# Tail scores of a sliding-window attention: row halves of the array trade their products, in another order of all engines

## The chip, the cores and the metric

The kernel runs on one core of a Trainium2 chip. The metric is the device time of one execution in microseconds (us). The engines are TensorE (PE; its weight loads are shown apart as PEld), VectorE (DVE), ScalarE (ACT), GpSimd (POOL), and SyncE (SP), which issues nearly all transfers.

## What is computed

An attention with a sliding window of 128 keys and a linear bias by distance, for 8 batches, 8 heads, 576 positions and a head width of 64; its output, 512 wide, goes through a layer of four causal attention experts of width 64, of which each position takes two. Cut to what matters:

```python
B, H, S, D = 8, 8, 576, 64
scores = scale * q @ k.T                       # per batch and head
mask = (rel >= 0) & (rel < 128)                # rel = query position - key position
scores = where(mask, scores + bias, -1e9)
x = softmax(scores) @ v                        # heads side by side: (B, S, 512)
logits = x @ w_gate                            # 4 experts, 2 taken
for e in range(4):                             # causal attention of width 64
    a = softmax(causal(scale * (x @ wq[e]) @ (x @ wk[e]).T))
    out += weight[e] * (a @ (x @ wv[e]) @ wo[e])
```

## The kernel before

**Groups.** Two heads of one batch are a group g, 32 of them (g = 4 x batch + pair). The first four run in another form (`half_s`, `half_tail` and what belongs to them); groups 4 to 31 run through `attn_s` (scores, softmax, scaling), `attn_t` (transposes of the probabilities) and `attn_pv` (attn·V). Out of the x that comes of it the expert layer computes projections (`qkproj`, `vproj`: tiles wx against WH and WL), causal scores (KKm against QHm, QLm, QJm), transposes, attn·V and the output product.

**Scores of a group.** The head width of 64 is the depth of a score product, so one product takes only 64 of the 128 rows of TensorE's array, and with 64 queries only 64 of its columns. Four such products can stand in the array side by side. The tile `w5` of a group (called `e` in `attn_s`) holds queries and keys of its first head on partitions 0 to 63 and those of its second head on partitions 64 to 127. The unit u = 0 makes two score tiles: `ss[0]`, the first head's, from partitions 0 to 63 (the lower row half of the array), and `ss[1]`, the second head's, from partitions 64 to 127 (the upper one). `products` gives each of them, per tile of 128 queries, two products of 64 queries: against 128 keys for the first query tile and against 192 for the others. The unit u = 1 does query tiles 2 and 3 in the same way.

**The tail.** 576 positions are four query tiles of 128 and a tail of 64. The tail's 64 queries of each head are multiplied with the last whole block of 128 keys and with the 64 keys behind it. In the kernel before, the lower half makes the two products of 128 columns (one for each head) into `ss[0]` and the upper half the two of 64 columns into `ss[1]`, recorded behind the other products of u = 0; a predicated copy on DVE lays the latter over a part of the former, and the tail's block of 128 x 128 goes to the softmax with the blocks of `ss[0]` (`part[0]`). So each half needs queries and keys of the head that the other one holds: `load_hi` fetches them by three small transfers of 64 partitions x 2 x 64, 64 x 128 and 64 x 64 values.

**attn·V.** `attn_pv` too goes by row halves: the keys of a block on partitions 0 to 63 are multiplied on the lower half, those on 64 to 127 on the upper one. Per head the lower half has 3 x 192 + 128 + 64 + 64 = 832 columns, the upper one 3 x 192 + 64 + 64 = 704.

**Order.** All of this is first recorded as a list of operations (`_Rec`). `plan` then writes it out in the order that a table, `ORDER`, gives: for each step the number of an operation and, where an operation may run on one of two engines (copies on ACT or DVE, roundings and scalings on POOL or ACT, subtractions on DVE or POOL), which one is taken. Products that share their place in the array by halves are kept together in pairs (`_pairs`). `place` gives the tiles their buffers, first come, first served, and L1189 issues all of it, so that nearly every instruction has that line. The semaphores follow from the buffers. A buffer number in a name (ps_75, w_84) is thus part of the order too: the same tile may have another number in the other kernel.

Of the kernel before, what the change touches and what calls it, by code (L numbers as in the profile page):

```python
# [19 lines left out]
B, H, S, D = 8, 8, 576, 64  # L20
DM = H * D
E = 4
P = 128
NP_ = H // 2
NQ = S // P
TAIL = S - NQ * P
# [3 lines left out]
SCALE = 1.0 / math.sqrt(D)  # L30
# [8 lines left out]
    "c-p;KeOO#sdB69bckVgKy_*?3v(C6PEBMS*Xc<c?bfFFvTIT7{9onHn1q&8jMnfAOVI35@ObZH?C_IHND7cB6)I>p{5*sSG@RU@dpu{B=Y_N$2g{NSHCKf"  # L39
    "6vY18-Id*=f-Yd`+z<zw#Lk8|GhzQ6bP{@x>q!mqqZIPsVeKYrOmGCYuFQ>%z-v8K{;h(b;Yo><!;<0MQmKgl4wblhq4x~Nh`ed(9xr+Q%|MU6nTiZGR#Z"  # L40
    "7iPxD*~#vIGGwEmPQ9aSsJs_AHUGCP}W}wETDQ)B1~=}&#Lq+yHpktsz@cXQCc6ORm?4aWJCUU#^8l_?ziudJWAZ&%sn)ub$`b*yz8`8vE}BG_JdXMusb-"
    "_LvrcPz*^=+Q*-n*tX%E31QzE??nQ6G{A6)p0ono+`TqQ}Ebzd4q>QgW$6oi`u@mcWhYz0rG9~OWcR>__Q?}BcE`VH^%wa7NJGh{}*LNcb#r-hQI1SJXD@"
    "%}@?-z19r}`|)!^OPGw!CwtMR=M;m~9H0ak(c!JI+!UovE;8Qk%nE&~$#}qJ^-D@_XKeIcEO^yc0qmfHeLfEn-&HM;FW!aB&3Y7=Q{z&=o4{^;Sb2^*IYX"
    "h1AJXoq1V#R<OIki7)M@tD(HCAYo>h@M!b3;N$_Afl2<`F?Myi+*PzQVqx=nFdQllK$hRvGwhnZUo(6;pjecd6JL7ZyleHW`qQW_)#vX9#Y0n$KjVM?qvh"
    "=ohWOD1XFBlLQu{|A*l7v*=m;a!#uT;zA%K4MDn7EeR8cbSFAliQ6xvevp%9<|^8I)tIL_YwsSo!3=DR+e>8F+9YSxbzRSI60O6}loQQOS7F0-58e(pX0q"
    "*AJy5g{3`{l<28O?Hbh`?}AcHxM)BBJ6FS>$Y`wo{yw5=LjKor=K=QoB2JGH$DL&5^)6V#ACJCQ=R9QW?a?9S87rr&Ff@smNQOv4P6V0y1r%g%vS(Z!b@)"
    "-4-buoVe-H#{}HQ!X|<%3%#1fwltLK}dZ!itH9@2#2z9mfZh%xL`j{%zqOj`#a{v!J+v*zBsnEHZxkBB@+9t&^WMNijv8p!OpK^Qd!j+jt!ft=(yEo6lbv"
    "TXBECd~maBX(9X>53Gtv*n^1);J~ruKTo^6=96hhYmupyp-|X(MdS`|D4+gBQ*YncL5%V^-RGm^(zRRTSuZ|8Ub6of@Cm+s8Mvl<1eg6meA`Lgq_T0hV9_"
    "Hem~6jW_XxkG`}5=g&-6=fZ{)!Of55ryl$KXIEFVa<lReKxrb)JJ-qT;=<QfM}H64!M@|MFJAe?r!3h4wSc|mgj&j)x`w{$Gj*E5Y&ENdq+1Gsdc4pB{X_"
    "le+$w<4>tW(v7=);+cH_=gv@KXx)!-<8ph3O%EMbhWE||h^v)2p#BtY1`-ZQmM$I5(5_sXW)<fWd`e&%H5iY<D6<oubuP*&7;al2z~f2VE@SS5SYQ`xo;z"  # L50
# [192 lines left out]
def attn_moe_kernel(ctx, tc, hd, rd, vd, wall, wo, mk, tb, tm, mt, ident, out):  # L243
    nc = _Rec()
# [1032 lines left out]
```

## Time and profile before

| what | us |
| --- | --- |
| median of 3 runs (lowest, highest) | 477.76 (477.13, 478.05) |
| the profiled execution's own time | 478.22 |
| its span in the trace | 476.4 |
| its time around the span | 1.8 |

The span runs from the first to the last instruction in the trace; the execution's own time holds some 1.8 us more around it. The mean granted clock of TensorE in it is 0.996 of full speed. All rows below are of this one execution.

### The profile page before, as it was taken

What the parts mean: (1) busy time and instruction counts of PE and PEld (TensorE: products, weight loads), DVE (VectorE), ACT (ScalarE), POOL (GpSimd) and SP (SyncE); (2) the same over time, 40 slices, a digit from 0 to 9 for tenths busy, and PEclk for the clock granted to TensorE, in tenths of its full rate; (3) what the DMA queues carried; (4) which work ended last, traced back from release to release, by engine and by line L of the source; (5) the groups of instructions that cost most, each with busy time, mean ns of one, the idle gap of its engine ahead of it and who ended that gap; (6) DMA issues with size and microseconds to landing.
All of it is one profiled execution on the core that took longest, in us unless ns stands there. A gap on an engine that the chain in (4) does not pass through costs nothing.

```text
span 476.4 us, 17537 instructions
## 1 busy us (share of the span) xinstructions
PE 468.2 (98%) x6380; PEld 409.5 (86%) x6380; DVE 410.3 (86%) x1900; ACT 371.0 (78%) x1416; POOL 218.2 (46%) x451
## 2 busy tenths in 40 slices
PE   7999999999999999999999999999999999999996
PEld 5888889897889788798898988998889897899875
DVE  6899999989998998879979898898998979975840
ACT  5867978978989577797987989498786968934962
POOL 4713779093826227243381626625163613352440
PEclk9899999999999999999999999999999999999999
DMA  8889333009136026160362047411733030300033
GB/s 200 263 206 225 89 110 80 7 2 221 49 104 141 2 68 192 34 161 1 87 174 68 1 116 192 119 27 38 167 94 102 4 85 2 119 1 1 3 111 111
DMA packets 29861, 44.98 MB, mean 94 GB/s; under 512 B 9424, under 2 KB 15824, under 8 KB 29776
## 3 DMA queue, kind: packets, MB, share of 16 engines
q1 hardware_dynamic: 29040, 43.42, 34.3%
q8 instruction: 50, 0.82, 0.7%
q10 hardware_dynamic: 736, 0.46, 0.4%
q14 instruction: 35, 0.29, 0.2%
HBM read 34.42 MB, written 9.44 MB: 92 GB/s over the span
## 4 chain that ended last, share of the span: by engine, by line
PE 80%; DVE 8%; DMA 4%; ACT 3%; SPq 2%; POOL 2%; issue 1%; DVEq 0%
PE ps L1189 80%; DVE w L1189 5%; ACT w L1189 2%; SPq L1189 2%; POOL w L1189 2%; DMA w<-in_hd 2%; DMA w<-in_rd 1%; DVE ps L1189 1%; DMA w<-in_wall 1%; DVE KKm L1189 0%; DVE r L1189 0%; DVE WL L1189 0%; DVE ALm L1189 0%; DVE mr L1189 0%; ACT QJm L1189 0%
## 5 line engine op out<-in xcount | busy, mean ns | idle before, releaser
L1189 ACT COPY w<-ps 128x512 f32<-128x512 f32 (+3 forms) x230 | 92.9, 449 | 31.1 <-PE ps L1189 20.1
L1189 PE MATMUL ps<-wx,WH 128*128 128x288 f32 (+2 forms) x512 | 110.6, 300 | 0.0
L1189 ACT ACTIVATE w<-w,nm 128x128 f32<-128x128 f32 x252 | 98.8, 395 | 7.5 <-DVE nm L1189 7.3
L1189 POOL TENSOR_SCALAR w<-w,r 128x128 f32<-128x128 f32 x165 | 60.6, 380 | 88.5 <-ACT w L1189 30.5
L1189 POOL TENSOR_SCALAR w<-w,mr,w 128x256 f32<-128x256 f32 (+3 forms) x128 | 78.2, 621 | 43.0 <-DVE mr L1189 15.8
L1189 PEld LDWEIGHTS ps<-wx,WH 128*128 128x128 f32 x512 | 83.3, 189 | 1.5 <-DVE mnm L1189 0.2
L1189 ACT ACTIVATE w<-w,mnm 128x256 f32<-128x256 f32 (+3 forms) x128 | 70.9, 557 | 14.4 <-DVE mnm L1189 13.0
L1189 DVE CUSTOM_DVE_ANT_0 w<-ps,tbt 128x128 f32<-128x128 f32 x288 | 72.5, 283 | 2.9 <-PE ps L1189 2.1
L1189 DVE TENSOR_TENSOR w<-ps,tmt 128x768 f32<-128x768 f32 (+3 forms) x96 | 72.4, 771 | 2.0 <-PE ps L1189 0.9
L1189 PE MATMUL ps<-wx,WL 128*128 128x288 f32 (+2 forms) x256 | 72.0, 296 | 0.0
L1189 PE MATMUL ps<-WH,wx 128*128 128x260 f32 x288 | 62.9, 287 | 0.0
L1189 PE MATMUL ps<-idt,w 64*128 64x64 f32 (+1 forms) x1152 | 60.4, 231 | 1.3 <-POOL w L1189 1.0
L1189 PE MATMUL ps<-w 64*64 64x192 f32 (+3 forms) x1256 | 58.9, 306 | 0.5 <-DMA w<-in_hd 0.4
L1189 PEld LDWEIGHTS ps<-idt,w 64*128 64x128 f32 (+1 forms) x1152 | 48.1, 139 | 11.4 <-issue 3.7
L1189 PE MATMUL ps<-w,vt 64*64 64x192 f32 (+4 forms) x1344 | 56.6, 284 | 0.4 <-ACT w L1189 0.4
L1189 PEld LDWEIGHTS ps<-w,vt 64*64 64x64 f32 (+1 forms) x1344 | 49.7, 133 | 6.5 <-ACT w L1189 1.0
L1189 DVE COPY_PREDICATED ps<-mkt,ps 128x128 f32<-128x128 int32 (+2 forms) x160 | 50.0, 329 | 2.4 <-PE ps L1189 2.0
L1189 PEld LDWEIGHTS ps<-w 64*64 64x64 f32 (+1 forms) x1256 | 45.0, 134 | 7.8 <-DMA w<-in_hd 1.6
L1189 DVE CUSTOM_DVE_ANT_0 w<-ps,mtt 128x384 f32<-128x384 f32 (+2 forms) x96 | 49.8, 551 | 1.0 <-PE ps L1189 0.6
L1189 PEld LDWEIGHTS ps<-WH,wx 128*128 128x128 f32 x288 | 48.4, 190 | 0.7 <-DVE nm L1189 0.2
L1189 PE MATMUL ps<-w,w 128*64 128x64 f32 (+4 forms) x576 | 48.2, 319 | 0.0
L1189 ACT ACTIVATION_READ_ACCUMULATOR w<-w,nm 128x1 f32 x252 | 48.2, 191 | 0.0
(110 smaller groups left out, 944.9 us busy)
## 6 DMA issues: line engine op xcount, KB each, us to landing
w<-in_hd SPq DMA_DIRECT2D x56, 288.0 KB, 4.7
vt<-in_vd SPq DMA_DIRECT2D x28, 320.0 KB, 4.3
out<-w SPq DMA_DIRECT2D x31, 256.0 KB, 2.7
w<-in_hd SPq DMA_DIRECT2D x14, 128.0 KB, 3.6
w<-in_hd SPq DMA_DIRECT2D x56, 32.0 KB, 3.9
w<-in_wall SPq DMA_DIRECT2D x4, 386.0 KB, 5.5
out<-w SPq DMA_DIRECT2D x8, 128.0 KB, 2.3
vt<-in_vd SPq DMA_DIRECT2D x4, 192.0 KB, 4.8
```

Source lines behind the costliest of these rows:

```text
L1189: getattr(getattr(tc.nc, e), m)(*a, **k)
```

## The change

In `attn_s` the two halves trade their tail products: the lower one now makes the two of 64 columns, into `ss[0]`, the upper one the two of 128 columns, into `ss[1]`. The predicated copy goes the other way, and the tail's block joins the blocks of `ss[1]`. In `load_hi` the three small transfers keep their sizes: the one of two pieces now goes to partitions 0 to 63, the other two go to 64 to 127. The table ORDER is another one throughout.

```diff
--- before.py
+++ after.py
@@ -36,79 +36,79 @@
 ORDER = (
-    "c-p;KeOO#sdB69bckVgKy_*?3v(C6PEBMS*Xc<c?bfFFvTIT7{9onHn1q&8jMnfAOVI35@ObZH?C_IHND7cB6)I>p{5*sSG@RU@dpu{B=Y_N$2g{NSHCKf"
...
+    "c-pmi4OAT2b!Jz++w~r*8dX`{p6;D)A8^2i7{-v$Ss23%*pPq+){p}Z*f0SHZ192&4rIZB2_%p}299A2UKB$tIZ`ZqL;{W&ix?*0fCDFJ1`@Oj8`u>yQY<"
...
 )
@@ -387,11 +387,12 @@
         r, vt = loaded.pop(g)
         a = hd[b, p]
         row = a.ap[0][0]
-        src = bass.AP(tensor=a.tensor, offset=a.offset + D * row + NQ * P, ap=[[row, D], [QW, 2], [1, TAIL]])
-        nc.sync.dma_start(r[D:, 2 * S : 2 * S + 2 * TAIL].rearrange("p (a n) -> p a n", a=2), src)
-        t = 2 * QW + S + P + (NQ - 1) * P
-        nc.sync.dma_start(r[:D, 2 * S + TAIL :], a[:D, t : t + P])
-        nc.sync.dma_start(r[:D, 2 * S : 2 * S + TAIL], a[:D, QW + S + P + TAIL : QW + S + 2 * P])
+        k1 = 2 * QW + S + P
+        q1 = QW + S + P + TAIL
+        src = bass.AP(tensor=a.tensor, offset=a.offset + q1, ap=[[row, D], [k1 + NQ * P - q1, 2], [1, TAIL]])
+        nc.sync.dma_start(r[:D, 2 * S : 2 * S + 2 * TAIL].rearrange("p (a n) -> p a n", a=2), src)
+        nc.sync.dma_start(r[D:, 2 * S + TAIL :], a[D:, QW + (NQ - 1) * P : QW + NQ * P])
+        nc.sync.dma_start(r[D:, 2 * S : 2 * S + TAIL], a[D:, NQ * P : S])
         prepped[g] = (None, None, None, vt, r)
 
     def warm():
@@ -418,16 +419,15 @@
         ss = [s_tile(g, u), s_tile(g, u + 3)]
         part = products(ss, 2 * u, [e[:, : NQ * P], e[:, TAIL:S]], e[:, S : 2 * S], tbt[:, p], 5)
         if u == 0:
-            c = slice(3 * P, 4 * P)
             lo, up = e[:D], e[D:]
             x, m = 2 * S, S + (NQ - 1) * P
-            nc.tensor.matmul(ss[0][:D, c], lo[:, NQ * P : S], lo[:, m : m + P], start=True, stop=True)
-            nc.tensor.matmul(ss[0][D:, c], lo[:, x : x + TAIL], lo[:, x + TAIL :], start=True, stop=True)
-            c = slice(3 * P, 3 * P + TAIL)
-            nc.tensor.matmul(ss[1][:D, c], up[:, x : x + TAIL], up[:, x + TAIL : x + 2 * TAIL], start=True, stop=True)
-            nc.tensor.matmul(ss[1][D:, c], up[:, :TAIL], up[:, m + P :][:, :TAIL], start=True, stop=True)
-            nc.vector.copy_predicated(ss[0][:, c], mkt[:, P:], ss[1][:, c])
-            part[0].append((3 * P, tbt[:, p, 4], -SCALE, 4))
+            c, w = slice(3 * P, 3 * P + TAIL), slice(3 * P, 4 * P)
+            nc.tensor.matmul(ss[0][:D, c], lo[:, NQ * P : S], lo[:, m + P :][:, :TAIL], start=True, stop=True)
+            nc.tensor.matmul(ss[0][D:, c], lo[:, x : x + TAIL], lo[:, x + TAIL : x + 2 * TAIL], start=True, stop=True)
+            nc.tensor.matmul(ss[1][:D, w], up[:, x : x + TAIL], up[:, x + TAIL :], start=True, stop=True)
+            nc.tensor.matmul(ss[1][D:, w], up[:, :TAIL], up[:, m : m + P], start=True, stop=True)
+            nc.vector.copy_predicated(ss[1][:, c], mkt[:, P:], ss[0][:, c])
+            part[1].append((3 * P, tbt[:, p, 4], -SCALE, 4))
         for h in range(2):
             wrap(ss[h], 2 * u)
             blocks(g, ss[h], part[h])
```

What the new table moves is shown at three places.

On PE, behind the last products of attn·V of group 7 (`w_92,vt_160`), stand the scores of group 8 (tile `w_84` before, `w_83` after). A row with x2 is two products of one half of the array: the two heads' in attn·V and in the tail, the two query halves' in the other scores. Before, ps_76 and ps_71 are tiles of the lower half, ps_73 and ps_75 of the upper one:

```order
L1189 MATMUL ps_72<-w_92,vt_160 64x64 x2
L1189 MATMUL ps_70<-w_92,vt_160 64x64 x2
L1189 MATMUL ps_76<-w_84 64x192 x2
L1189 MATMUL ps_73<-w_84 64x192 x2
L1189 MATMUL ps_76<-w_84 64x192 x2
L1189 MATMUL ps_73<-w_84 64x192 x2
L1189 MATMUL ps_71<-w_84 64x192 x2
L1189 MATMUL ps_75<-w_84 64x192 x2
L1189 MATMUL ps_71<-w_84 64x128 x2
L1189 MATMUL ps_75<-w_84 64x128 x2
L1189 MATMUL ps_71<-w_84 64x128 x2
L1189 MATMUL ps_75<-w_84 64x64 x2
```

After, ps_75 and ps_72 are tiles of the lower half, ps_69 and ps_71 of the upper one:

```order
L1189 MATMUL ps_70<-w_92,vt_160 64x64 x2
L1189 MATMUL ps_76<-w_92,vt_160 64x64 x2
L1189 MATMUL ps_75<-w_83 64x192 x2
L1189 MATMUL ps_69<-w_83 64x192 x2
L1189 MATMUL ps_75<-w_83 64x192 x2
L1189 MATMUL ps_69<-w_83 64x192 x2
L1189 MATMUL ps_72<-w_83 64x64 x2
L1189 MATMUL ps_71<-w_83 64x128 x2
L1189 MATMUL ps_72<-w_83 64x192 x2
L1189 MATMUL ps_71<-w_83 64x192 x2
L1189 MATMUL ps_72<-w_83 64x128 x2
L1189 MATMUL ps_71<-w_83 64x128 x2
```

The tail's pairs have changed sides: 64x128 ended the lower half's list before (`ps_71`) and 64x64 the upper one's, and now the 64x64 stands on the lower half (`ps_72`) and the 64x128 on the upper one (`ps_71`), both ahead of the other products of their tiles.

On PE, behind the expert scores of batch 0 (KKm), stands attn·V of group 6 (`w_90,vt_155`). Before:

```order
L1189 MATMUL ps_74<-KKm,QLm 128x384
L1189 MATMUL ps_72<-KKm,QLm 128x384
L1189 MATMUL ps_74<-KKm,QHm 128x384
L1189 MATMUL ps_72<-KKm,QHm 128x384
L1189 MATMUL ps_76<-w_90,vt_155 64x192 x2
L1189 MATMUL ps_73<-w_90,vt_155 64x192 x2
```

After:

```order
L1189 MATMUL ps_70<-KKm,QHm 128x512
L1189 MATMUL ps_74<-KKm,QHm 128x512
L1189 MATMUL ps_71<-KKm,QHm 128x384
L1189 MATMUL ps_72<-KKm,QHm 128x384
L1189 MATMUL ps_73<-wx_79,WH 128x320 x2
L1189 MATMUL ps_73<-wx_79,WL 128x320
L1189 MATMUL ps_76<-w_90,vt_155 64x192 x2
L1189 MATMUL ps_69<-w_90,vt_155 64x192 x2
```

Three products of the projections (`wx_79`), of 320 columns each, now stand between the two.

On SP, at the start, the second half of the first groups' inputs (`w_91`) and the tail keys of group 4 (`w_82`, `w_83` before, `w_89` after) are fetched. Before:

```order
L1189 DMA w_91<-in_rd 128x2x320
L1189 DMA w_91<-in_hd 128x2x128
L1189 DMA w_91<-in_hd 64x2x256 x2
L1189 DMA vt_129<-in_vd 128x384
L1189 DMA vt_128<-in_vd 128x384
L1189 DMA w_82<-in_hd 64x64
L1189 DMA w_83<-in_hd 64x2x64
```

After:

```order
L1189 DMA w_91<-in_rd 128x2x320
L1189 DMA w_91<-in_hd 128x2x128
L1189 DMA w_89<-in_hd 64x64
L1189 DMA w_91<-in_hd 64x2x256
L1189 DMA w_89<-in_hd 64x128
L1189 DMA w_91<-in_hd 64x2x256
L1189 DMA w_89<-in_hd 64x2x64
L1189 DMA vt_129<-in_vd 128x384
L1189 DMA w_89<-in_hd 64x1152
```

Two of the three small fetches of the tail have moved ahead of the last piece of `w_91`, the third stands right behind it.

## Rows read from the trace of the kernel before

**Rows 1.** Head of the page: the span, and busy time by engine.
```profile
span 476.4 us, 17537 instructions
...
PE 468.2 (98%) x6380; PEld 409.5 (86%) x6380; DVE 410.3 (86%) x1900; ACT 371.0 (78%) x1416; POOL 218.2 (46%) x451
```

**Rows 2.** Waits of PE: who was waited for: us in total, times, longest.
```profile
PE ps L1189 <- DVE ps L1187: 1.3, 1, 1.3
PE ps L1189 <- POOL w L1189: 1.0, 2, 0.7
PE ps L1189 <- ACT w L1189: 0.4, 1, 0.4
```

**Rows 3.** Waits of PEld, the weight loads, in the same columns.
```profile
PEld ps L1189 <- ACT w L1189: 4.3, 15, 0.7
PEld ps L1189 <- POOL w L1189: 3.4, 12, 0.9
```

**Rows 4.** Timeline of PE, four places: start us, busy us, line, operation, shape, count.
```profile
34.64 1.63 PE L1189 MATMUL ps<-w 64*64 64x128 f32 x40
36.20 1.21 PE L1189 MATMUL ps<-w,vt 128*64 128x64 f32 x18
...
185.85 1.64 PE L1189 MATMUL ps<-w,vt 64*64 64x192 f32 x44
187.42 0.33 PE L1189 MATMUL ps<-idt,w 128*128 128x128 f32 x1
...
258.02 2.39 PE L1189 MATMUL ps<-w 64*64 64x128 f32 x64
261.81 0.54 PE L1189 MATMUL ps<-wx,WH 128*128 128x288 f32 x2
...
414.97 3.07 PE L1189 MATMUL ps<-w,vt 64*64 64x192 f32 x88
417.97 0.33 PE L1189 MATMUL ps<-idt,MPL 128*128 128x128 f32 x1
```

**Rows 5.** Timeline of PE, 202.3 to 203.2 us.
```profile
202.78 0.38 PE L1189 MATMUL ps<-w 64*64 64x192 f32 x2
202.83 0.22 PE L1189 MATMUL ps<-w,vt 64*64 64x64 f32 x2
202.89 0.55 PE L1189 MATMUL ps<-w 64*64 64x192 f32 x8
```

**Rows 6.** Timeline of PE, 62.5 to 67.5 us; in brackets idle time ahead and its releaser.
```profile
62.57 0.45 PE L1189 MATMUL ps<-wx,WH 128*128 128x320 f32 x2
62.86 0.31 PE L1189 MATMUL ps<-wx,WL 128*128 128x320 f32 x1
...
64.90 0.35 PE L1189 MATMUL ps<-KKm,QHm 64*128 64x384 f32 x2
65.61 1.99 PE L1189 MATMUL ps<-w,vt 64*64 64x192 f32 x44 [0.36 <-ACT w L1189]
```

**Rows 7.** Lines by form, POOL: count, busy us, mean ns of one, idle time before.
```profile
L1189 POOL TENSOR_SCALAR w<-w,r 128x128 f32<-128x128 f32 x165 | 60.6, 380 | 88.5 <-ACT w L1189 30.5 <-DVE r L1189 27.4 <-PE ps L1189 14.6
```

**Rows 8.** Timeline of SP (issues of transfers), from 13.5 us.
```profile
14.27 1.96 SPq L1189 DMA_DIRECT2D w<-in_hd  x3
```

**Rows 9.** Chain that ended last, its start: start us, us, what.
```profile
13.84 6.93 DMA w<-in_rd
```

**Rows 10.** Timeline of PE, 27 to 29.9 us.
```profile
27.81 1.95 PE L1189 MATMUL ps<-w 128*128 128x192 f32 x34
```

**Rows 11.** Timeline of POOL, 349 to 358 us.
```profile
352.66 4.21 POOL L1189 TENSOR_SCALAR w<-w,mr,w 128x128 f32<-128x128 f32 x6
```

**Rows 12.** Timeline of PE, 353.5 to 358 us.
```profile
356.39 1.21 PE L1189 MATMUL ps<-idt,w 64*128 64x64 f32 x23 [0.26 <-POOL w L1189]
```

**Rows 13.** Timeline of PE, 70.5 to 75 us.
```profile
71.07 1.64 PE L1189 MATMUL ps<-w,vt 64*64 64x192 f32 x44
...
74.35 0.66 PE L1189 MATMUL ps<-KKm,QJm 128*128 128x288 f32 x3
```

More of the change, by code (lines that the diff above doesn't have):

```diff
@@ new lines @@
+    "&h9YiF?Z-EXG|dr*glp9P4|AVh=C@!F~>>Vmo36%k_aEog)GmiCs9!k^ukyiLk*9WQvmyOtHPmSuzVlo-~I`!N#ho9(|1tRBpZk*nNr&Z1IB358`RIAGPC"
+    "kYmu|tQFWmhfq!LjnB+;vdFbmMi^t(#AtRB#YiqmAx3gqL4>E=$D$K9M;L*(cEHC<01h)>{^Rs$hnC2PmuIld0rVR25N&=JAM_3OSt~&tHB^J?s9)MDOxI"
+    "n9Zk4ZmJsY6lUTKdjH{QjVGdxO#I%=T0O|4BDPVR-kmH4&qfANcB;jzi?oMbK5_xMqwhZ?@>zRaXte7ms*cUM0CnYp3{W64bk)4^$IdAV7$ci~&VRa@Q4v"
+    "chT89Y<zl0!=CLCg*vt4VufQ_}7o{0JKCqR(m|KHRS~ws}VJZg2$Pi8b1jdz7)eYI!V`9B26)RBa7KTf6rKTfu>arF0bYuvBTRqAUBK4Q^3b&XFzJ@Fr@z"
@@ new lines @@
+    "9zkKbRMeIsrLK3Ldt?De|zh<?(URPcDy}#bQrp2-`n1#9NIDm#}`g`C0?khM|qi~0!Ux=pX*2d559PU&^u-Wa+h{@?udds0)0H~Y8aYd!~9^A{GhbA=}YK"
+    "of1uMYs(PPvjRWPS2oWsUmD1oXx}@o7dr^Es#?WOp4B<2syu-L!$Zhx!Ta>}ef|_3eR2yGO{Pw*$kx7#uuEoB;c?FasykbGD<|1t7BvuWBEgo~tY?+e|OG"
+    "Ia&iPh0%rDW3chf9^mI__$nMeJ{%rBWJf3IdATevGflg@V>}|nJFa~C{V&)5zMZVDk*O{i0k{TKC0++ius{A}k^RE;!Y*!Pv~&q|6P<zM4lbFMeq*8~$rq"
+    "KE&Z?(Zn<{(mZN7C2++BqA(-?fe*h|Rx1Z`azg`A4gEE>MGLU#v;Mpz5$O%E^2X{>S7(g?LJst|3Gq7^`PzWU;S(;iMF@R-6FgyBa(A3ki(@j&f_&OZG9-"
@@ new lines @@
+    "zL8@KQ|m+&l)f%+i}#-zL0Fih$2^DzUi&fr#w-_Rj+k<8xU2B%$Lvq7{Aa=%0&tl{nm`VeV%_u{vfOE*-VIK<f80$AT&5_;Oj9*Ua<yrBb;<YQ9OQ?Kn~;"
+    ")hM=jncJx!wspc|Na5i*;nrKQi9Sfxt>Lb=LW4rnz4Q{-d<@d{u-UbK6D+yl!S8kqxV3NRb0U#+gt(8QkmQ_}b78IY%h4(^c8sU?c0M_Y!Bbr1l(UpirzV"
+    "=o8cy`?MZbuO~R#{qCXB*h6G7=&@OuLKkW*BJ)*LK_S33IA!ba-KU!{wqhrN!CW<)zh!I3zC-va5FKy>i{_*ypK%H6TaD&@Rk5f!6=^IxR~mss);o&dR9M"
+    "Xq<%IhrqTm@bs0t2AXb%%W;k45E$xcyQ(tP33~anwD<S5_7>`Ue0U-86Hc9y`l9?SNKcOE-a-cfg!7qImj`z5Uwj=_HvUHc9TMee8DtJhyIDm!J9^KXT7v"
@@ new lines @@
+    "17`kL~ue+!gf{oFsoW_nZuoB$ABl-dBn78>i&Y0#x>m81#~TFXiQI@DHy>(LvZ%=pN&b%rB4L3a^q#OSdkGpjK60n9$?$v;S_nsI1Q#<pP}9s^hY=;-*!c"
+    "EmHgja$4Kpoa{yCf!|wFQ;x6)B036g5%i*Rz%2ct^~g#m*&~7_W1C`d=Pnj;Os0dIBLIEeIEhqL2?xuCrUji%+FPeDdhF_0$G@KX8w<tzEb+FhmfhWCqG3"
+    "Uq`pDhxjNI(T;pQLH(|_NdKTazJo=8phBxLs<^0JB?7RhgF7Nl{12p|3e9f!JT`~GwAKyl}hkF3{3*JNRM=~L+>$_Iwn`5`uVFR<|?`Lj~-kcn!hn{t|J+"
+    "sJ8VEe|GKJ@JP_otT}Hz#&B*mJJb#65_VzxN5g7TVjU9_Vfd)f`bj`pFZQ5}3#6?Md&u48;Y;%0T+Ou?4fYmW|bUGD8-zK-JeTc5)+Xd}Ez0mM(7GNZejt"
@@ L112 @@
+    "fqZnDI#XOXytgI6FfuGsm&hTG4$}7iYz4Zf8=bMS0fteQzYr9wn+b<u73sfV!uW"
 )
```

127 lines of the change are left out of this document (55 added, 72 removed).

## The prediction

> **What bounds the kernel now.** I read the head of the page first. In a span of 476.4 us PE is busy for 468.2 us (98%), while POOL is busy for 46% [rows 1]. Then I read who keeps PE waiting: the longest entry of its list, 1.3 us in one wait, lies before the first product; behind it come 1.0 us for POOL and 0.4 us for ACT [rows 2]. The list for the weight loads, which mostly run behind products, adds 4.3 us for copies of ACT and 3.4 us for scalings of POOL, in 27 waits [rows 3]. So the time is that of the work on PE, in the order in which it stands there; another engine counts only where PE catches up with it. A change can pay in two ways: the products themselves take less time on PE, or one of these few waits goes. It can cost by making new ones.
>
> **How long the products of half the array take.** Scores and attn·V of a group use 64 of the 128 rows of the array at a time, and two streams run side by side: the lower half (rows 0 to 63) and the upper half. The next product that takes all rows has to wait for both. I looked up stretches that hold nothing but such products, and took their length from the start of the first to the start of the next full one [rows 4]. By the code, the scores of one group have 128 + 192 + 192 + 192 + 128 = 832 columns on the lower half and 768 on the upper; attn·V of one group has 832 and 704.
> - Scores of one group, 34.64 to 36.20: 1.56 us.
> - attn·V of one group, 185.85 to 187.42: 1.57 us.
> - attn·V of two groups, 414.97 to 417.97: 3.00 us.
> - Scores of one group, the first unit of a second one, and attn·V of one, 258.02 to 261.81: 3.79 us; 832 + 448 + 832 = 2112 columns below, 768 + 384 + 704 = 1856 above.
>
> From the second and third, 832 columns more below cost 1.43 us, which is 1.72 ns per column with 0.14 us to begin and end. The fourth would then be 2112 x 1.72 ns + 0.14 = 3.77 us (measured 3.79), and the first 1.57 (measured 1.56). Had the upper half set the time, 704 columns more would cost 1.43 us, 2.03 ns each, the first would be 1.57 + 64 x 2.03 ns = 1.70 and the fourth 3.91. So the longer half sets the time, and before the change that is always the lower one: attn·V leans on it by 128 columns and the tail of the scores by another 64.
>
> **The change part by part.** *The tail products.* The lower half gives up 64 columns per tail and the upper half takes them. In a stretch without attn·V this only swaps which half is longer. Where attn·V stands in the same stretch, the longer half gets shorter by 64 columns, 64 x 1.72 ns = 0.110 us. I counted both orders on PE: each has 60 stretches of half-row products between full ones. Of the 28 tails, 7 stand in a stretch without attn·V, before as after. Of the other 21, two meet an attn·V whose last products stand in another stretch, so that half of the excess is missing there and the tail only turns it round. 19 tails remain: the longer halves of all stretches sum to 19 x 64 = 1216 columns less. If all of it shows, that is 19 x 0.110 = 2.09 us.
>
> Whether all of it shows depends on how far the halves can run apart. In 12 of the 19 the tail stands ahead of the attn·V that it makes up for: the lower half is simply done earlier and takes the next product, which is next in order anyway. In 7 it stands behind: the upper half must have run ahead of the lower one by the time the tail comes. A row shows that it can: at 202.78 two score products start, the others not before 202.89, while the lower half is still at attn·V (202.83) [rows 5]. The order on PE names the two of the lower half first, so the two early ones are those of the upper half, 0.11 us ahead of their turn. How much of such a lead lasts through a whole group no row shows; between 0 and 0.110 us I take half, 0.055. The sum is 12 x 0.110 + 7 x 0.055 = 1.70 us, with the ends 1.32 (no lead lasts) and 2.09 (all of it).
>
> The Trainium skill has a rule on either side. "TensorE: Matmul & The Clock Gate", The mechanism, says that products start and end strictly in the order of the program, whatever tile they use; by it the 7 give nothing and the sum is 1.32. "TensorEngine Tiling (Array Packing)", Key Properties, says that tiles operate independently; by it the sum is 2.09. The rows at 202.78 speak against the first as a strict rule.
>
> *The wait of attn·V at 65.61.* PE starts the last score product of batch 0 at 64.90 and then sits idle for 0.36 us until the copies of group 6's transposes are there [rows 6]. In the new order three products of 320 columns stand in this place. Two of them took 0.29 us (62.57 to 62.86) [rows 6], so three cover 0.44 us, which is all of the idle time. They are taken from where PE did not wait, so I count 0.36 us of gain; the lower end is 0, should the copies be later by as much.
>
> *The fetches and the rest.* The three tail fetches keep their sizes (16, 32 and 32 KB); only partitions and offsets change. Likewise the predicated copy keeps its 128x64 shape, and the tail's block moves from the first score tile's list to the second's with the same instructions. All of it lies beside PE, and costs nothing so long as PE's rows above stay without a wait on DMA or DVE. *Engines.* POOL gets 13 instructions more, 12 of them scalings that ACT did: 12 x 0.380 = 4.6 us [rows 7] on an engine that idles for 54% of the span. DVE and ACT lose 6 and 7. That, too, costs nothing on average; what it can cost at a place is a rival below.
>
> *The start.* On SP, two small tail fetches of group 4 now stand ahead of the last piece of the first groups' inputs. Three issues took 1.96 us [rows 8], so two are 1.3 us, and the last piece, the third of that row, moves from about 15.6 to 16.9. The slowest transfer there took 6.93 us [rows 9], which puts its landing at 23.8 at the latest. Before, the products on it started inside the row of 27.81 [rows 10]; by the order they now stand some 2 us of PE work earlier, at about 26. The cover is 2 us; without it PE would wait for each us by which the landing is later. I take 0.
>
> Sum: 478.22 (this profiled execution) - 1.70 - 0.36 = 476.16 us. The median of the runs is 0.46 below this execution, so I forecast **475.7 us**.
>
> **The rivals.** *Strict order between the halves.* No lead lasts, and the 7 tails behind give nothing: 477.76 - 1.32 - 0.36 = 476.1. For it: the lead at 202.78 is only 0.11 us, and nothing shows it later. Against it: the same rows. Chance 0.18. By the first rule of the Trainium skill named above this is the case to come.
>
> *New waits take the gain back.* The order of all engines is another one, and PE catches up at other places. Before, ACT and POOL held up products and weight loads for 9.1 us in 30 waits, 0.3 us each [rows 2, 3]. Four to six more of them cost 1.2 to 1.8 us: 476.9 to 477.5, not to be told from before (a difference under 0.2%, 0.96 us, is none that a measurement of this kernel tells). For it: the slack of transposes and attn·V behind their copies is small in both orders. Against it: the sequence of large blocks on PE is nearly the same. Chance 0.20.
>
> *POOL's queue holds up the transposes: slower.* POOL works in order, and a transpose waits for the last scaling of its block. At 352.66 six scalings in a row took 4.21 us [rows 11], and PE came to wait for them at 356.39 [rows 12]. With 12 scalings more in the queue this would have to happen at ten further places of 0.3 us each before 2.06 us of gain turn into a loss of 0.96 us; from 3.0 us of new waits on, the kernel is slower, around 479. For it: POOL is the engine that gets more work. Against it: it idles half the time, and ahead of the same transposes the new order leaves out two of the long roundings. Chance 0.08.
>
> *Waits go elsewhere too.* If one us of the remaining waits goes as well, 474.7. Chance 0.09.
>
> **How the numbers follow.** The forecast has 0.45 and its own range is 475.2 to 476.3, strict order 0.18, waits that eat the gain 0.20, slower 0.08, a larger gain 0.09. Faster by over 0.2% means below 476.8: 0.45 + 0.18 + 0.09 = 0.72. Within 0.2%: 0.20. Slower: 0.08. The range leaves out the slower case and about half of the larger gain, and takes in that of new waits: 474.5 to 477.7.
>
> **What the profile after would show.** The tail: the stretch near 71 to 74 us, attn·V of group 7 and scores of group 8 (3.28 us before [rows 13]), gets shorter by about 0.1 us, and stretches of scores alone keep 1.56 us. The sum over all such stretches falls by 1.3 to 2.1 us at an equal number of products. The wait at 65.61: no idle time of PE ahead of attn·V of group 6. The start: no wait of PE on these fetches between 24 and 30 us. Wrong would be the forecast if the half-row stretches keep their lengths (then the halves are bound to each other), or if PE's list of waits on ACT, POOL or DMA grows by more than 1 us.

## The result and the profile after

| | before | after |
| --- | --- | --- |
| median of 5 runs, us (those of before beside the change) | 477.13 | 472.78 |
| lowest, highest | 476.61, 478.05 | 471.57, 474.09 |
| profiled execution, us (its span) | 478.22 (476.4) | 473.2 (471.4) |

The ratio is 0.9915, with an interval of 0.9896 to 0.9933: the change is faster by 4.35 us. The forecast was 475.7, a gain of 2.06; the result lies below its range. The sign was right; the size that was forecast was half of what came.

First the head of the page of the changed kernel, which answers to [rows 1].

```profile
span 471.4 us, 17542 instructions
...
PE 462.7 (98%) x6380; PEld 403.8 (86%) x6380; DVE 409.3 (87%) x1894; ACT 370.5 (79%) x1409; POOL 222.7 (47%) x464
```

PE is as full as before, with the same 6380 products: its busy time fell by 5.5 us and the span by 5.0. The time was thus not won in idle time of PE that the profile lists as such. Next the waits of PE after the change, in the columns of [rows 2].

```profile
PE ps L1189 <- DMA w<-in_hd: 1.7, 3, 0.7
PE ps L1189 <- DVE ps L1187: 1.3, 1, 1.3
PE ps L1189 <- POOL w L1189: 0.9, 2, 0.5
PE ps L1189 <- DVE w L1189: 0.4, 1, 0.4
```

The wait for ACT is gone. PE's wait for fetched inputs of the scores (DMA) has grown to 1.7 us in three pieces; before it was

```profile
PE ps L1189 <- DMA w<-in_hd: 0.4, 2, 0.2
```

The longest of the three after the change stands ahead of a tail product, in the timeline of PE around 284 us:

```profile
284.45 0.60 PE L1189 MATMUL ps<-w 64*64 64x128 f32 x10 [0.67 <-DMA w<-in_hd]
```

The waits of the weight loads after the change, as in [rows 3]:

```profile
PEld ps L1189 <- POOL w L1189: 3.4, 11, 0.7
...
PEld ps L1189 <- DMA w<-in_hd: 2.7, 6, 0.8
PEld ps L1189 <- ACT w L1189: 2.4, 9, 0.4
```

Those for ACT fell from 4.3 us in 15 to 2.4 us in 9; POOL's stayed, in spite of its 4.5 us more work. The whole list did not fall: leaving out "issue", it sums to 18.5 us before and 20.9 after.

Last the places that the prediction named, in the timeline of PE after the change:

```profile
33.20 1.64 PE L1189 MATMUL ps<-w 64*64 64x192 f32 x40
34.77 0.44 PE L1189 MATMUL ps<-w,vt 128*64 128x128 f32 x4
...
63.03 0.31 PE L1189 MATMUL ps<-wx,WL 128*128 128x320 f32 x1
63.27 1.47 PE L1189 MATMUL ps<-w,vt 64*64 64x192 f32 x28
...
68.96 1.58 PE L1189 MATMUL ps<-w,vt 64*64 64x192 f32 x42
...
71.97 0.40 PE L1189 MATMUL ps<-wx,WH 128*128 128x288 f32 x1
```

Scores alone take 34.77 - 33.20 = 1.57 us, as before [rows 4]. attn·V of group 6 starts at 63.27 with no idle time in brackets ahead of it, where it waited 0.36 us [rows 6]. attn·V of group 7 with the scores of group 8 takes 71.97 - 68.96 = 3.01 us, where it took 74.35 - 71.07 = 3.28 [rows 13]: 0.27 less, not 0.1.

To see where the time went I cut PE's whole course into the 60 stretches of products that use 64 rows at a time (scores, attn·V, and the transposes and causal scores that stand among them; these are the stretches of the prediction) and the rest, each from its first start to the next one's. These sums are made from all starts in the trace, in us. The last four are kernels of the experiments below.

| kernel | stretches of 64 rows | the rest | together |
| --- | --- | --- | --- |
| before | 171.2 | 299.5 | 470.7 |
| after | 167.2 | 298.8 | 466.0 |
| before, with fillers (e4) | 170.8 | 298.5 | 469.3 |
| after, with fillers (e8) | 166.0 | 298.3 | 464.3 |
| e8, tail widened (e12) | 167.5 | 298.7 | 466.2 |
| before, only the tails traded (e1) | 172.8 | 299.8 | 472.6 |

The stretches got 4.0 us shorter; 1.3 to 2.1 was forecast. The profiled execution of before also lost about a microsecond at its start to a halved clock, which is not in that of e4; the two filled kernels are therefore the cleaner pair: 4.8 us out of 5.0 lie in the stretches, and the rest of PE's work takes what it took.

### The profile page after: what moved, and what is told of

The parts are those of the page before. It is cut to its first block, busy times and chain, and to the rows that moved or that the text cites. A ratio compares the mean times of both kernels' runs of the same rounds, so it can differ in the third digit from the quotient of the medians.

```text
span 471.4 us, 17542 instructions
## 1 busy us (share of the span) xinstructions
PE 462.7 (98%) x6380; PEld 403.8 (86%) x6380; DVE 409.3 (87%) x1894; ACT 370.5 (79%) x1409; POOL 222.7 (47%) x464
## 4 chain that ended last, share of the span: by engine, by line
PE 84%; DMA 5%; SPq 3%; DVE 3%; ACT 2%; POOL 1%; issue 1%; DVEq 0%
PE ps L1189 84%; DMA w<-in_hd 4%; SPq L1189 3%; DVE w L1189 2%; ACT w L1189 2%; POOL w L1189 1%; DMA w<-in_wall 1%; DVE ps L1189 1%; DVE WL L1189 0%; DVE ALm L1189 0%; ACT AHm L1189 0%; DVE mr L1189 0%; DVE nm L1189 0%; POOL QJm L1189 0%; DVE ALTm L1189 0%
## 5 line engine op out<-in xcount | busy, mean ns | idle before, releaser
L1189 ACT COPY w<-ps 128x256 f32<-128x256 f32 (+2 forms) x232 | 92.4, 443 | 29.8 <-PE ps L1189 21.3
L1189 POOL TENSOR_SCALAR w<-w,r 128x128 f32<-128x128 f32 x177 | 64.6, 378 | 68.3 <-PE ps L1189 25.4
L1189 ACT ACTIVATE w<-w,mnm 128x512 f32<-128x512 f32 (+3 forms) x128 | 71.2, 558 | 10.0 <-DVE mnm L1189 9.4
L1189 PE MATMUL ps<-WH,wx 128*128 128x260 f32 x288 | 61.5, 285 | 0.0
L1189 PE MATMUL ps<-idt,w 64*128 64x64 f32 (+1 forms) x1152 | 58.6, 230 | 1.0 <-POOL w L1189 0.9
L1189 PE MATMUL ps<-w,vt 64*64 64x192 f32 (+3 forms) x1344 | 56.3, 283 | 0.0
L1189 PEld LDWEIGHTS ps<-w 64*64 64x64 f32 (+1 forms) x1256 | 44.0, 134 | 8.6 <-DMA w<-in_hd 2.7
L1189 DVE CUSTOM_DVE_ANT_0 w<-ps,mtt 128x256 f32<-128x256 f32 (+2 forms) x96 | 49.8, 551 | 0.8 <-PE ps L1189 0.4
```

The lines of the kernel that those rows point to most:

```text
L1189: getattr(getattr(tc.nc, e), m)(*a, **k)
```

## The experiments

My theory after the result: the tail products give what was forecast, and the other half of the gain is time in which PE stands inside its stretches because another engine's data or buffer is late, which the new order takes away. The rivals: the tail is worth twice my price; the gain comes from the start; it comes from the clock.

**e4_fill and e8_after_fill: the clock.** PE had been idle in part between 10 and 12 us. Filler products of 256 columns, whose result nobody reads, are put there, six before and five after. In the table's entries (operation, engine chosen; -2 is a filler), that of before:

```diff
 (79, 0)
+-2
 (78, 0)
+-2, -2, -2, -2
 (82, 0), (110, 0)
+-2
```

> Before, with six more filler products (128x256, results unused) on PE between the first three transposes, 9.5 to 11.3 us, where PE has nothing to do; no other instruction moves. If the idle time ahead of it is why the clock falls: the clock stays at 1.0 from 10 to 16 us and the time is 477.1 - 1.6 = 475.5 us. If the clock falls for another reason, or costs nothing there: 477.1 us, or up to 0.3 us more where the fillers delay the transposes.

> The changed kernel with five more filler products on PE between the first three transposes, as in e4_fill. In 2 of 5 runs of the change the granted clock was 0.996, which in runs of before goes with about 1.1 us more. If that is the same fall of the clock at the start: no run at 0.996, the median at 472.0 to 472.5 us. If it comes from elsewhere: 472.8 us and the same spread.

Measured: e4 476.76 us, ratio 0.9993 (0.9984 to 1.0002); e8 471.57, ratio 0.9882 (0.9869 to 0.9895). The windows of 2 us in the kernel before, with busy time of PE, PEld, DVE, ACT and POOL, the granted clock, the share of the DMA engines and GB/s:

```profile
10.00:12.00 2.00, 1.14 (x5) 0.83 (x5) 1.79 (x16) 1.84 (x10) 1.88 (x6) 0.90 0.80 230
12.00:14.00 2.00, 2.00 (x13) 1.67 (x14) 1.38 (x8) 2.00 (x11) 0.72 (x2) 0.50 1.01 331
```

The same windows of e4:

```profile
10.00:12.00 2.00, 1.73 (x13) 1.52 (x13) 1.93 (x17) 1.88 (x10) 1.99 (x6) 1.00 0.85 255
12.00:14.00 2.00, 2.00 (x39) 1.68 (x37) 1.74 (x14) 2.00 (x11) 0.75 (x3) 1.00 0.90 293
```

With PE busy for 1.14 of the 2 us, the granted clock of the next window was 0.50 (1.2 GHz of 2.4) and PE got through 13 products; with 1.73 busy it stayed at 1.00 and got through 39. But this fall is in some executions only: e4 is no faster than the median of before, since most executions of before lack it (last section). So the clock explains how widely the runs of one kernel lie apart, and not the gain: between kernels without the fall it is 476.76 - 471.57 = 5.2 us. (The two ran beside different runs of before, with medians of 476.89 and 477.07.) e8 is faster than both kernels.

**e12_wide: the price of the tail.** In e8 the two lower tail products get 128 columns again, 64 of which nobody reads; order, engines and fetches stay (the predicated copy reads the 64 that count). The lower half is then as long as before the change.

```diff
-nc.tensor.matmul(ss[0][:D, c], lo[:, NQ * P : S], lo[:, m + P :][:, :TAIL], ...)
-nc.tensor.matmul(ss[0][D:, c], lo[:, x : x + TAIL], lo[:, x + TAIL : x + 2 * TAIL], ...)
+nc.tensor.matmul(ss[0][:D, w], lo[:, NQ * P : S], lo[:, m + TAIL : m + P + TAIL], ...)
+nc.tensor.matmul(ss[0][D:, w], lo[:, x : x + TAIL], lo[:, x : x + 2 * TAIL], ...)
```

> The change with fillers (e8_after_fill, 471.57 us), the same order, buffers and results, but the lower half's tail products have 128 columns again, of which 64 are junk that nobody reads. The longer halves of all stretches grow by 1216 columns, back to before's sum. If the halves run apart freely: 471.6 + 2.1 = 473.7 us. If a tail behind attn·V gives nothing: 472.9 us. If the tail's columns lie beside other work: 471.6 us.

Measured: 473.18 us, ratio 0.9915 (0.9901 to 0.9929), 1.61 more than e8. In the table above the stretches grow by 1.5 us. Two of them in the timeline of PE in e8:

```profile
68.61 1.58 PE L1189 MATMUL ps<-w,vt 64*64 64x192 f32 x42
...
71.61 0.40 PE L1189 MATMUL ps<-wx,WH 128*128 128x288 f32 x1
...
253.67 0.99 PE L1189 MATMUL ps<-w 64*64 64x64 f32 x24
...
257.21 0.40 PE L1189 MATMUL ps<-wx,WH 128*128 128x288 f32 x1
```

and in e12:

```profile
68.82 1.58 PE L1189 MATMUL ps<-w,vt 64*64 64x192 f32 x42
...
71.83 0.40 PE L1189 MATMUL ps<-wx,WH 128*128 128x288 f32 x1
...
254.78 0.99 PE L1189 MATMUL ps<-w 64*64 64x128 f32 x24
...
258.53 0.40 PE L1189 MATMUL ps<-wx,WH 128*128 128x288 f32 x1
```

The second stretch holds two tails and grows from 3.54 to 3.75 us, 0.10 for each. The first holds one, behind all of attn·V, and keeps its 3.00. Over all stretches, start by start: the seven tails without attn·V change nothing (0.00 each). Of the 12 that stand ahead, 11 change their stretch by 0.09 to 0.10. Of the 7 counted as behind, four have the last products of attn·V still to come (per head 128 columns on the lower half and 64 on the upper one) and give 0.10 to 0.11 as well; the one with nothing of attn·V behind it gives 0.00, like the two whose attn·V ends in another stretch. (Three share a stretch with another stall, and can't be read.) So the rival that the tail is worth twice the price falls.

**e1_tail and e2_order: one half of the change each.** e1 keeps the table of before and trades only the tails, with the fetches and the predicated copy; e2 has the table of the change with the tails of before. In each one copy on ACT stands earlier, since a score tile lives longer there.

```diff
+nc.vector.copy_predicated(ss[1][:, c], mkt[:, P:], ss[0][:, c])
...
+            if u == h == 0:
+                blocks(g, ss[1], [(3 * P, tbt[:, p, 4], -SCALE, 4)])
```

(e1; it leaves the tail's softmax steps where they stood, behind the first head's.)

> The order of before, with only the tail products of the two halves traded (the tail's softmax block stays at its place in the order, and one copy on ACT stands earlier, since a score tile now lives longer). The sum of the longer halves falls by the same 1216 columns as in the change. If the halves run apart freely: 477.1 - 2.1 = 475.0 us, and the attn·V and scores stretch near 71 us falls from 3.28 to about 3.05 us. If they start strictly in the order of the program: 475.8 us. If the tail gives nothing by itself and the whole gain of the change is in its order: 477.1 us. The start to 16 us stays as before in each case, with the granted clock at half in 12 to 14 us.

> The changed order with the tail products of before (one copy on ACT stands earlier, since a score tile lives longer). If the tail is worth 2.1 us, the order alone has the other 2.2 us of the 4.35: 474.9 us, with the granted clock at 1.0 through the first 20 us. By the prediction's own steps the order is worth 0.36 us: 476.8 us. If order and tail need each other: above 477.

Measured: e1 479.72 us, ratio 1.0053 (1.0041 to 1.0065); e2 479.00, ratio 1.0044 (1.0029 to 1.0058). Both are slower than before, though together they make 4.35 us of gain. The waits of the weight loads in e1:

```profile
PEld ps L1189 <- ACT w L1189: 5.2, 18, 0.7
PEld ps L1189 <- DVE nm L1189: 3.9, 13, 0.7
```

The entry for `nm`, a small tile that DVE makes out of the scores in a step of the softmax, is new at that size: as I read it, products wait until DVE has read a score tile and its buffer is free. The stretches grew by 1.6 us where the tails alone should have cut 1.6, so some 3.2 us of standing came in (against e4 it is 3.6). The waits of PE in e2:

```profile
PE ps L1189 <- DVE KKm L1189: 1.7, 1, 1.7
...
PE ps L1189 <- DVE nm L1189: 1.3, 5, 0.3
```

Here too DVE is late, but mostly elsewhere: e2's stretches sum to 169.4 us, 1.4 less than e4's, and the rest to 302.1, 3.6 more. So the new order shortens the stretches with the old tails too, and loses more outside them. Neither half of the change gains by itself.

**e3_start: the start.** Before, with its first 141 steps in the order of the change; 111 of them move.

```diff
-(10, 0), (19, 0), (18, 0), (7, 0), (16, 0)
+(4, 0), (9, 0), (7, 0), (12, 0), (10, 0)
```

> Before, with only the operations of its first 141 steps (on PE up to the second half's scores of groups 0 and 1, about 16 us) put in the relative order that they have in the change. Theory of the clock: in the profile of before the granted clock is at half from about 11.6 to 14.9 us, which costs 1.6 us; in the new start it stays at 1.0, so 477.1 - 1.6 = 475.5 us, and the scores at 13.93 take 1.46 us in place of 1.97. Theory of the prediction (the start gives 0): 477.1 us, whatever the clock does, since the start waits for data.

Measured: 476.95 us, ratio 0.9999 (0.999 to 1.0008). The start gives nothing and takes nothing.

**e5_mirror, e6_unmirror and e7_mid: other orders of the softmax steps.** e5 is e1 with the softmax steps of the two heads traded as well, in 283 entries of the table; e6 does the reverse to e2; e7 is before with the 543 entries of the steps from 45 to 81 us in the order of the change.

```diff
-(431, 0), (424, 0), (440, 0), (449, 0)
+(424, 0), (431, 0), (440, 0), (449, 0)
```

(e5 against e1, the first place.)

> The order of before with the tail products traded, as in e1_tail, but the softmax steps of the unit's two score tiles trade places in the order too, so that the tile which holds the tail keeps the place, and so the lifetime of its buffer, that it had in before. Theory of the lifetimes (what e1_tail lost, it lost in waits for score buffers that are read longer, and the shorter half of the array is a gain): 476.9 - 2.1 = 474.8 us if the halves run apart, 475.6 us if they start strictly in the program's order, with waits on DVE as in before. Rival (trading the halves costs by itself in before's order): 479 us or more, as e1_tail.

> The changed order with the tail products of before, as in e2_order, but with the softmax steps of the unit's two score tiles traded in place, so that the lifetimes of the buffers stay those of the change. If the tail is worth 2.1 us in this order too: 472.8 + 2.1 = 474.9 us, so that the order alone keeps 2.0 us of the gain. If the order without the tail is worth nothing, or costs: 477 us or more. If the tail is worth nothing: 472.8 us.

> Before, with only the operations between 45 and 81 us (steps 545 to 1101) put in the relative order that they have in the change; tail products as before. From the two profiles: the time beyond what the products need falls from 3.7 us in that part to 2.4 us, so 476.9 - 1.3 = 475.6 us. By the step of the prediction (only the wait of 0.36 us goes): 476.5 us. If what is saved there comes back later: 476.9 us.

Measured: e5 479.67 us, ratio 1.0057 (1.0044 to 1.0071); e6 475.78, 0.9965 (0.9952 to 0.9979); e7 481.19, 1.0074 (1.0058 to 1.0089). In all three the new places put the step that reads the softmax sums ahead of the exponentials that make them, for 13 blocks in e5, 8 in e6 and 1 in e7, so that these kernels leave out a wait that the others have. Their times therefore decide nothing on the tails, and nothing below rests on them.

**e9_mid, e10_late and e16_last: which part of the program.** Before with fillers, with the change's order, choice of engines and traded tails in one part: e9 from 45 to 81 us (groups 6 to 8), e10 from 81 us to the end (groups 9 to 31), e16 from 216 us (groups 19 to 31).

```diff
+SWAPPED = (9, 10, 11, 12, 13, 14, 15, 16, 17, 18, 19, 20, 21, 22, 23, 24, 25, 26, 27, 28, 29, 30, 31)
...
+        if g in SWAPPED:
```

(e10; the new lines of the tail stand under it, the old ones under `else`.)

> Before with the six fillers of e4_fill (476.76 us), and with the part from 45 to 81 us as the change has it: the operations of steps 545 to 1101 in the change's relative order, and the tail products of groups 6, 7 and 8, which lie wholly inside, traded. The longer halves fall by 2 x 64 columns there, 0.22 us. If the stalls of PE in that part go as the two profiles show it (3.7 us beyond what the products need, 2.4 us after): 476.8 - 0.2 - 1.3 = 475.3 us. By the step of the prediction (only the idle time of 0.36 us goes): 476.2 us. If it comes back later: 476.8 us.

> The complement of e9_mid: before with the fillers, and everything from 81 us on as the change has it, with the tail products of groups 9 to 31 traded. The longer halves fall by 17 x 64 columns, 1.87 us if all of it shows. With the stalls that the profile of the change with fillers lacks from 100 us on (1.6 us): 476.8 - 1.9 - 1.6 = 473.3 us, and e9_mid and e10_late together make the 5.2 us between e4_fill and e8_after_fill. By the prediction (the tails alone, 17 of its 19): 475.2 us.

> e10_late with a later border: before with fillers up to 216 us, from there on the change, with the tails of groups 19 to 31 traded (10 x 64 columns of the longer halves). If the gain is spread evenly over the stretches: tails 10 x 0.085 to 0.110 us, 0.9 to 1.1, and some 1.0 us less of stalls, 474.6 to 474.9 us. If it hangs on one place between 81 and 216 us: 475.8 us or more.

Measured: e9 481.17 us, ratio 1.0085 (1.007 to 1.0101); e10 473.07, 0.9912 (0.9899 to 0.9926); e16 475.40, 0.9966 (0.9954 to 0.9977). e9 misses: it is 4.4 us slower than e4. At its first seam, where one order passes into the other, PE stands for 2.0 us, as its timeline shows; the rest of the loss was not followed:

```profile
47.96 0.33 PE L1189 MATMUL ps<-idt,w 128*128 128x128 f32 x1 [1.43 <-ACT w L1189]
48.82 0.41 PE L1189 MATMUL ps<-wx,WH 128*128 128x320 f32 x1 [0.53 <-ACT w L1189]
```

The other two have one seam each. Against e4 e10 gains 3.7 us and e16 1.4, and e8 gains 1.5 beyond e10. Of the 5.2 us, 1.5 lie before 81 us, 2.3 between 81 and 216, and 1.4 behind. By e12 a tail that counts gives 0.10: 17 such tails stand behind 81 us and 10 behind 216. That leaves about 2.0 us of other gain behind 81 us, 0.4 of it behind 216, and 1.4 before 81, where one such tail stands. It is not at one place. How it divides behind 81 us is rough: what the seams of e10 and e16 cost is not known, e16's runs lie 1.6 us apart, and its median stands between the two cases that were expected.

**e11_three: the gap at attn·V of group 6.** Before with fillers; only the three products of 320 columns (891 to 893) move from ahead of the causal scores to the gap that the prediction wanted them to fill, and the two reads of their result (894, 895) with them.

```diff
 (1028, 0)
-(891, 0), (892, 0), (893, 0)
 (1029, 0)
-(894, 0), (895, 0)
 (685, 0), (686, 0), (684, 0), (681, 0), (679, 0), (683, 0), (680, 0), (682, 0)
...
 (750, 0), (751, 0), (752, 0)
+(891, 0), (892, 0), (893, 0)
```

> Before with the fillers, and with only the three 320-column products moved behind the scores of batch 0, ahead of attn·V of group 6 (the two reads of their result move behind them). By the prediction's step the idle time of 0.36 us goes: 476.4 us. If the new neighbours only move the wait, since the scores ahead of it come earlier by as much: 476.8 us. If the stall is the 0.6 us between the starts beyond a product's own time: 476.2 us.

Measured: 478.51 us, ratio 1.0028 (1.0017 to 1.0039), 1.75 more than e4. The timeline of PE in e11:

```profile
63.92 0.44 PE L1189 MATMUL ps<-KKm,QHm 64*128 64x384 f32 x1 [0.42 <-ACT w L1189]
64.64 0.56 PE L1189 MATMUL ps<-wx,WH 128*128 128x320 f32 x2
65.04 0.31 PE L1189 MATMUL ps<-wx,WL 128*128 128x320 f32 x1
65.28 0.54 PE L1189 MATMUL ps<-w,vt 64*64 64x192 f32 x4
66.39 0.39 PE L1189 MATMUL ps<-w,vt 64*64 64x192 f32 x4 [0.57 <-DVE KKm L1189]
```

The three products came where they should, and attn·V starts behind them without a wait. But 0.42 us of waiting for ACT now stands ahead of the last causal scores, and attn·V waits behind its first products, 0.57 us for DVE's step on KKm. That step is the second of the two moved reads: DVE does it at 65.84 us in e11. So part of the new waiting is made by the edit. The run shows that three products in the gap gain nothing in before's order; it does not show what keeps this place clean in the change.

**e13_eng_after, e14_eng_before and e15_evac_after: the choice of engines.** The two tables differ in the chosen engine of 307 operations: 150 copies out of PSUM (72 from ACT to DVE, 78 the other way), 118 scalings (53 from POOL to ACT, 65 back), 31 roundings and 8 subtractions. e13 is e8 with before's choice in all of them, e15 with before's choice in the 150 copies, e14 is e4 with the change's choice.

```diff
-(82, 1), ... (104, 1), ... (106, 1)
+(82, 0), ... (104, 0), ... (106, 0)
```

(e13, the first three of 307.)

> The change with fillers (471.57 us), every instruction at its place in the order, but each of the 307 copies, roundings, scalings and subtractions for which the change takes another engine than before goes to the engine that it had in before. If the choice of engines is what spares PE its stalls (in the lists of waits the weight loads wait 4.3 us for ACT before and 2.4 us in the change): 471.6 + 1.9 to 3.2 = 473.5 to 474.8 us. If the order alone spares them: 471.6 us. If order and choice fit only together: above 475 us.

> The reverse: before with fillers (476.76 us), the order and the tails as they are, with the change's choice of engine for the same 307 instructions. If the choice by itself spares the stalls: 476.8 - 1.9 = 474.9 us or less. If the order alone does: 476.8 us. If they fit only together: above 477.5 us.

> As e13_eng_after, but only the 150 copies out of PSUM go back to the engine (ACT or DVE) of before; the 118 scalings and 31 roundings stay as in the change. PE waits for these copies, not for the roundings: if the choice counts, this run has most of what e13_eng_after loses. If the scalings count (12 more of them on POOL): 471.6 us.

Measured: e13 532.66 us, ratio 1.1176 (1.1161 to 1.1192); e14 549.49, 1.1523 (1.1507 to 1.1539); e15 504.76, 1.0589 (1.0574 to 1.0603). The waits of PE in e13, and then in e14:

```profile
PE ps L1189 <- POOL w L1189: 13.2, 12, 2.6
PE ps L1189 <- ACT w L1189: 7.2, 5, 2.7
```

```profile
PE ps L1189 <- ACT w L1189: 12.7, 11, 3.4
PE ps L1189 <- POOL w L1189: 12.3, 8, 5.6
```

The same work, in the same order, on engines that are busy for 46 to 87% of the span in e4 and e8, costs 33 to 73 us more when the choice does not belong to the order. Part of this is PE's clock: its mean granted share was 0.98 in the profiled execution of e13, 0.97 in e14 and 0.99 in e15. e13 and e14 come out as order and choice fitting only together, and e15 with about half of e13's loss; none says what share of the change's gain the choice has.

## Why the prediction was right in sign and wrong in size

**The tail products: right in size, one term of it by luck.** The sum was 1.70 us, with 1.32 and 2.09 as its ends; e12 measures 1.6 by the medians and 1.5 by the stretches. The rule behind it (the longer half sets the time) holds stretch by stretch: 0.00 where attn·V is absent, 0.10 for a tail that counts (0.110 forecast). The half price for the 7 tails behind attn·V stood for a lead of the upper half that lasts in part. No run shows such a lead. Of attn·V's 128 columns of excess on the lower half, 64 lie in its last products, and six of the 7 tails have these still to come: they stand ahead of what they make up for, like the 12. The seventh ends the stretch near 71 us, the place that I had named for the reader; it gave nothing, and the 0.27 us there are a stall that went. So the term came right in sum by luck. The Trainium skill's "TensorE: Matmul & The Clock Gate", The mechanism, has products start and end strictly in the order of the program; the tail that ends its stretch agrees with it (3.00 us in e8 and 3.01 in e12), and the four others can't speak against it, since the lower half's excess comes after them. What does speak against it as a rule for single starts is the 0.11 us of [rows 5]. The 1.32 us worked out from it had counted all 7 as giving nothing.

**The waits: the step that failed.** "They are taken from where PE did not wait, so I count 0.36 us of gain" was the only stall in the sum, and of the engines it said "That, too, costs nothing on average". Measured, the gain besides the tail is 5.2 - 1.6 = 3.6 us in the kernels with fillers. The term for stalls was too small by a factor of ten. Two things were wrong in how I came to it.

The first is how I read the profile. I took the waits of the weight loads to run mostly behind products. In stretches of half-row products many of them do not. Here is attn·V of group 6 in e4, first in the timeline of PE, then in that of PEld:

```profile
64.30 1.99 PE L1189 MATMUL ps<-w,vt 64*64 64x192 f32 x44 [0.37 <-ACT w L1189]
66.22 0.79 PE L1189 MATMUL ps<-idt,w 64*128 64x64 f32 x16
```

```profile
64.30 0.19 PEld L1189 LDWEIGHTS ps<-w,vt 64*64 64x64 f32 x4 [0.69 <-ACT w L1189]
64.86 1.28 PEld L1189 LDWEIGHTS ps<-w,vt 64*64 64x64 f32 x40 [0.37 <-DVE w L1189]
```

The 0.37 us ahead of 64.30 are listed for PE. But the group then takes 66.22 - 64.30 = 1.92 us where it needs 1.57: the weights of its fifth product were late by 0.37 us, and PE counts as busy meanwhile. The same 44 products in e8:

```profile
62.95 1.68 PE L1189 MATMUL ps<-w,vt 64*64 64x192 f32 x44
64.56 1.04 PE L1189 MATMUL ps<-idt,w 64*128 64x64 f32 x17
```

They take 1.61 us with no wait ahead: 0.37 + 0.31 = 0.68 us gained where I had counted 0.36. Another such place is attn·V with the transposes behind it, where POOL was late [rows 12]. In e4:

```profile
352.72 1.64 PE L1189 MATMUL ps<-w,vt 64*64 64x192 f32 x44
354.42 0.28 PE L1189 MATMUL ps<-idt,w 64*128 64x64 f32 x2
354.95 1.21 PE L1189 MATMUL ps<-idt,w 64*128 64x64 f32 x23 [0.26 <-POOL w L1189]
355.92 0.51 PE L1189 MATMUL ps<-wx,WH 128*128 128x288 f32 x2
```

and in e8:

```profile
348.29 1.64 PE L1189 MATMUL ps<-w,vt 64*64 64x192 f32 x44
349.86 1.51 PE L1189 MATMUL ps<-idt,w 64*128 64x64 f32 x25
351.12 0.52 PE L1189 MATMUL ps<-wx,WH 128*128 128x288 f32 x2
```

3.20 us became 2.83, again more than the 0.26 in brackets. The better reading was at hand before: set each stretch against the price per column from clean ones, and the difference is the standing time, whoever the list names. The clean stretches give 0.14 us to begin, 1.72 ns per column of the longer half for scores and attn·V, 0.98 ns per column of a half for transposes and 0.47 ns for causal scores. By these prices the stretches behind 20 us stand 6.9 us above their price in e4, 3.7 in e8 and 3.3 in e12. e12 has the columns of e4 in the order of the change and with its choice of engines, so these two together take away 3.6 us of standing time. That is the size of the gain besides the tail.

Three stretches of e4, at 53.17, 61.93 and 352.72 us, hold 2.75 of its 6.9 us, and in them the weight loads waited 2.6 us for ACT, DVE and POOL. There the standing time and the waits for late data are about equal. For the rest the cause is argued from these three: the list of the weight loads as a whole, without "issue", sums to 17.7 us in e4 and 19.2 in e8, so many of its waits must have cost nothing.

The second thing is the engines. I took the net numbers of the order's counts (12 scalings more for POOL), but 307 operations change engine, in both directions. That is no small edit: taken alone it costs 61 to 73 us. What share of the 3.6 us hangs on it no run shows. "*New waits take the gain back*" and "*Waits go elsewhere too*" were priced at a third of a microsecond a wait and one microsecond in all; the second of them was the case that came, with 0.09.

**The mechanism at 65.61: not shown.** The wait is gone in the change, but in e11 the same three products in the gap come with other waits (0.42 and 0.57 us) and a loss of 1.75. So even the 0.36 us rest on a step that no run bears out.

**The fetches and the start: right at the start, incomplete behind.** e3 shows nothing at the start, as counted. Not foreseen were the longer waits for fetches later on (1.7 us in three where before had 0.4, the longest ahead of a tail product). In the profile of e8 they come to 0.7 in two, so they do not belong to every execution. The sign that I had set for a wrong forecast was PE's waits on ACT, POOL or DMA growing by over 1 us: those on DMA did, by 1.3, while the three together grew from 1.8 to 2.6. It was no good sign, for the time fell by more than was forecast. POOL's queue, the slower rival, did not come: PE waits for POOL for 0.9 us, before for 1.0.

**Open.** Which of the order's moves take the 3.6 us away was not separated further than by parts of the program (e10, e16): at e9's first seam the mixed order brought new waits, and neither the tails, nor the order, nor the choice of engines gained when taken alone (e1, e2, e13 to e15).

## What to carry to other kernels

Where short products wait for weights, PE counts as busy while it stands: compare each stretch with its price from a clean stretch before calling stalls small. When a change brings a new order, count how many operations change their engine, not by how many the engines' totals differ, and keep a wide range on the far side of the forecast too. Here the order, its choice of engines and the tails it was made for had no price of their own, each by itself.

## What the runs showed of the hardware

In the profiled execution of before the granted clock was 0.50 between 12 and 14 us. Of 59 timed executions of before beside the experiments, 17 show a mean clock of 0.995 to 0.996 and took 477.65 to 478.51 us (median 477.95); the other 42 show 0.997 or more and took 476.31 to 477.22 (median 476.82). The two lie 1.1 us apart; that all 17 had this same fall at the start is inferred, since they were not traced. With the fillers no execution of e4 (11) or e8 (4) shows such a mean; e9, which has them too, shows 0.996 in 2 of 4, not traced either. The two halves of the array are looser than one strict queue in single starts (0.11 us ahead of turn, [rows 5]), but no lead was carried through a group: 64 columns less on the lower half were worth 0.10 us where it had more to do later, and 0.00 at the end of a stretch.
